# Stores and job loads of one stage issued from GpSimd's DMA queue instead of SyncE's, in a gated FNet and Mish kernel

## The chip, the cores and the metric

The kernel runs on one core of one Trainium2 chip. The metric is the device time of one execution in microseconds (us). Three runs of the kernel before took 877.42, 878.73 and 881.01 us, so the median is 878.73 us.

## What is computed

The input `x` has 2048 rows of 640 columns, float32. One branch mixes it with Fourier matrices, the other is a dense layer, Mish and a second dense layer. A gate per row joins them:

```python
g = _sigmoid((x * gate_w).sum(-1, keepdims=True))
# branch A
a = jnp.einsum("bsd,ed->bse", x, dft_hid_re)
b = jnp.einsum("bsd,ed->bse", x, dft_hid_im)
y = jnp.einsum("ts,bse->bte", dft_seq_re, a) - jnp.einsum("ts,bse->bte", dft_seq_im, b)
# branch B, F = 1728
h = jnp.einsum("bsd,df->bsf", x, w1) + b1
act = h * jnp.tanh(softplus(h))
b = jnp.einsum("bsf,fd->bsd", act, w2)
return g * a_branch + (1 - g) * b
```

## The kernel before

**Arithmetic.** Each float32 operand is split into a high part (a copy on ScalarE, `copy`, L96) and a low part (a subtraction on VectorE, `tt`, L93), both in fp32r. A product is three matmuls of 128x128 by 128x512 (`mm3`, L107): high by high, high by low, low by high. The matrix products use Strassen-like block sums, so VectorE also adds and subtracts blocks of the operands and of the results.

**Stages.** The whole work is one list of `steps`, each of some 3 to 25 matmuls, built in Python in this order: the product with the sequence matrices (`seq`), the product with the hidden Fourier matrices (`hid`), the first dense layer, the second dense layer (`out`). The first dense layer, here "dense first stage", is steps `nd` = 336 to `n_dense` - 1 = 429. Counted in the order of the program, where the matmuls stand in the trace too, it is the matmuls 2,280 to 3,009 of 3,757. It starts with 13 steps of `dense_quads` (L866) and 8 of `dense_rest` (L768), then come two rounds of `dense_first` (L932), one for each half of the rows. `dense_quads` writes partial results to scratch tensors in device memory (names `p1_...`, `p2_...`, in the trace `p`), `p_load` (L973) reads them back some steps later. The activations go to the scratch tensors `act` and `actr`, and the `out` stage reads them.

**What a step needs.** A step names operands to load (`raw`), and preparations (`preps`, the split). The loop at L1239 goes through the steps. At step i it first issues the loads of operands of steps a few ahead (L1250; in the dense stages 6 steps for the preparation and 4 more for the load), then the preparations, then the matmuls of step i, then the stores that are due (L1259), and then whatever jobs fit.

**Jobs.** Work that isn't bound to one step stands in a list `jobs`, in a fixed order: low parts of weights, the gate, sums of blocks of `x` (`x_sum_jobs`, L855), weights of the dense layers (`quad_job` L660, `w1_job` L695), the multiplication of the Fourier branch by the gate (`yg`), the multiplication of the last activations by 1 - g (`aq`), weights of the second layer. A job has a load part and a work part. The loads are issued by the loop at L1286 when buffers are free, from the step `first` on at the earliest. The work part begins some steps later (L1282), and goes on as long as a planned clock of VectorE is behind a planned clock of TensorE by a margin (L1279). The six jobs of `x_sum_jobs` each load four blocks of `x`, make four sums on VectorE and store them to scratch tensors (`xs`, `q0s`, `q1s` in the trace); the dense first stage loads them as operands. Their `first` is `XS_FIRST + XS_EACH * n`, so 160, 168 and so on to 200. The trace has their first store at 285 us, in step 185.

**Buffers.** `FS` holds 22 tiles `f` of 128x512 float32 (256 KB), `FX` four tiles `fx` of 128x640, `W` the split weights, `R` the split operands. `Slots.get` takes the tile that has been free longest. A tile that is stored goes back to the list as soon as its store is issued in the plan; whoever takes it next then waits on the chip for that store to land. The Tile framework puts in these waits, and those for data, as semaphores.

**Queues.** Nearly all DMAs are issued by SyncE (SP), in the order in which the plan reaches them: operands at L1250, stores at L1259, loads of jobs into `fx` tiles at L154 (`fx_load`) and L692 (`quad2_load`), loads of jobs and of partial results into `f` tiles at L159 (`fs_load`) and L244 (`top_load`). SP works through its instructions in order: a store whose tile VectorE has not finished, or a load whose tile is not free yet, holds up all that stand behind it. ScalarE issues two loads at the start and one store near the end. GpSimd (POOL) issues no DMA and computes next to nothing.

Of the kernel before, what the change touches and what calls it, by code (L numbers as in the profile page):

```python
# [12 lines left out]
S, D, F = 2048, 640, 1728  # L13
P = 128
# [25 lines left out]
P2_LOAD, C_SEED = 4, 4  # L40
OPS0, OPS1 = (2, 7, 9, 11), (-4, 0, 2, 4, 5, 6, 8)
YG_FIRST, NO_LOAD = 18, 3
LATE_Y = (0,)
XS_FIRST, XS_EACH = 160, 8
R0, R1 = (2, 4), (2, 4)


# [14 lines left out]
def fnet_mish_gate(ctx: ExitStack, tc: tile.TileContext, xn, xt, c_re, c_im, wd_re, wd_im,  # L62
                   w1a, w1b, b1a, b1b, w2, gw, out):
    nc = tc.nc
# [13 lines left out]
    def scratch(name, n, rows=P):  # L78
        return [[dr.tile([rows, N], F32, name=f"{name}{i}_{t}") for t in range(TG)] for i in range(n)]

    usc, ysc = scratch("u", 2 * KD), scratch("y", KD)
    g_row, q_row = (dr.tile([1, S], F32, name=n) for n in ("g", "q"))
    gsc, qsc = ([r[:, t * N:(t + 1) * N].to_broadcast([P, N]) for t in range(TG)] for r in (g_row, q_row))
    asc = scratch("act", FC) + [[dr.tile([FR, N], F32, name=f"actr_{t}") for t in range(TG)]]

    clock = {"pe": 0.0, "dve": 0.0, "step": 0}
# [31 lines left out]
    A2, B2 = slice(0, 2 * P), slice(2 * P, 4 * P)  # L118
# [9 lines left out]
    def at(i, fn):  # L128

        events.setdefault(i, []).append(fn)  # L130
# [14 lines left out]
    def simple(fn):  # L145
# [3 lines left out]
            yield  # L149
        return work  # L150

    def fx_load(src, width=D):
        f = FX.get()
        nc.sync.dma_start(f if width == D else f[:, :width], src)  # L154
        return f

    def fs_load(src):
        f = FS.get()
        nc.sync.dma_start(f[:src.shape[0]], src)  # L159
        return f  # L160

    def job_load(i):
        j = jobs.pop(0)
        loaded.append((j, j.load(), i))

    def job_start():
        j, a, _ = loaded.pop(0)
        running.append((j.key, j.work(*a)))

    def job_go():  # L170
        key, work = running[0]
        pause = next(work, None)
        if pause is None:
            running.pop()
            done_jobs.add(key)
        return pause or 0
# [60 lines left out]
    def stage_jobs(st, order):  # L237
        def do_top(k, g):
            top(st, k, g[:, :3 * P])
            FS.put(g)  # L240

        def top_load(k):
            g = FS.get()
            nc.sync.dma_start(g[:, :3 * P], st.row(k)[:, :3 * P])  # L244
            return [g]

        for what, k in order:
            if what == "top":
                jobs.append(Job((st.kind, "top", k), simple(lambda g, k=k: do_top(k, g)),
                                lambda k=k: top_load(k), (st.kind, k) not in tops, fs=1))  # L250
            else:
                jobs.append(Job((st.kind, "low", k), lambda g, f, k=k: low(st, k, g, f),
                                lambda k=k: [fx_load(st.row(k + st.kh)), fs_load(st.row(k)[:, P:])],
                                2 + (k % KD == 0) + ((st.kind, k) not in tops), 1, 1))
            tops.add((st.kind, k))
# [82 lines left out]
    class Problem:  # L338
# [52 lines left out]
        def second(self):  # L391
# [96 lines left out]
            if self.out:  # L488
                for t in (t1, t2):
                    at(n - 2, lambda t=t: QT.update({t: fs_load((gsc if t in LATE_Y else qsc)[t])}))  # L490
                self.y_load(done - 5, t2, 4)
# [111 lines left out]
        def give(self, d, t, f):  # L603
            if self.out:
                y = YT.pop((d, t))
                if t in LATE_Y:

# [81 lines left out]
    def quad2_load(g):  # L689
        f = FX.get()  # L690
        for i in range(2):
            nc.sync.dma_start(f[:, i * 2 * P:(i + 1) * 2 * P], w1a[2 * g + i][:, B2])  # L692
        return [f]

    def w1_job(f, ga, gb):  # L695
# [440 lines left out]
    def put_u(m):  # L1136
        return lambda d, t, f: store(usc[m * KD + d][t], f, f)
# [9 lines left out]
    hid = Stage("hid", KD, lambda k: (wd_re, wd_im)[k // KD][k % KD], neg=True)  # L1147
    fin = Stage("out", FP, lambda k: w2[k * P:(k + 1) * P])

    def aside(name):  # L1150
        return [dr.tile([P, N], F32, name=f"{name}{j}") for j in range(3)]

    sq = [Problem(seq, q // 2, lambda t, k, m=q % 2: (c_re, c_im)[m][t, k], put_u(q % 2), q == 3,
                  aside(f"ps{q}") if q in (1, 2) else None) for q in range(4)]
    hd = [Problem(hid, tp, lambda t, k: usc[k][t], put_y, tp == 1, aside("ph") if tp else None) for tp in range(2)]
    ou = [Problem(fin, tp, lambda t, k: asc[k][t], put_out, False, aside("po") if tp else None) for tp in range(2)]

    unwritten.update(id(d) for p in problems for d in p.s2)

# [7 lines left out]
    def yg_jobs(*ts):  # L1167
        for t in ts:
            for d in range(KD):
                jobs.append(Job(("yg", t, d), simple(lambda *a, t=t, d=d: gate_y(t, d, list(a))),  # L1170
                                lambda t=t, d=d: ([fs_load(gsc[t])] if d == 0 else []) + [fs_load(ysc[d][t])], fs=2))

    def aq_jobs():
        for t in (3, 2):
            jobs.append(Job(("aq", t), simple(lambda *a, t=t: act_q(t, *a)),
                            lambda t=t: [fs_load(d) for d in (qsc[t], asc[FC - 1][t], asc[FC][t])], fs=3))

    yg_jobs(*[t for t in (0, 1) if t not in LATE_Y])
    aq_jobs()
# [18 lines left out]
    nd = len(steps)  # L1198
# [12 lines left out]
    narrow.update(range(nd, len(steps)))  # L1211
    quiet = set(range(nd - 4, nd + QUIET)) | set(range(nm + QUIET_A, nm + QUIET_M))
    n_dense = len(steps)
    no_load = set(range(n_dense - 3, n_dense + NO_LOAD))
    ou[0].first(ks=range(3))
    ou[1].first()
# [16 lines left out]
    def spare(i, job=False):  # L1233

        return SPARE + (SPARE_D * job if i in narrow else (i >= n_dense) * SPARE_OUT) + sum(takes.get(i + j, 0) for j in range(5))
# [3 lines left out]
    for i in range(n_all):  # L1239
        clock["step"] = i  # L1240
        while ready < n_all and ready <= i + (LEAD_D if ready in narrow else LEAD):
            while li < len(loads) and loads[li][0] <= ready + (AHEAD_D if loads[li][0] in narrow else AHEAD):
                n, (key, src) = loads[li]
                if n > ready and len(FS.free) <= spare(i):
                    break
                if id(src) in unwritten or id(src) in late and n >= n_dense and late[id(src)] not in done_jobs:
                    assert n > ready, (n, ready, i, key)
                    break
                f = RAW[key] = FS.get()
                nc.sync.dma_start(f[:src.shape[0], :src.shape[1]], src)  # L1250
                li += 1
            for prep in steps[ready][1]:
                prep()
            ready += 1
        clock["dve"] = max(clock["dve"], clock["pe"] - 3)
        steps[i][2]()
        while stores and stores[0][3] <= i:
            dst, v, f, _ = stores.pop(0)
            nc.sync.dma_start(dst, v)  # L1259
            FS.put(f)  # L1260
            unwritten.discard(id(dst))
        if steps[i][3]:
            steps[i][3]()
        for fn in events.get(i, ()):
            fn()
        if i == nm + GIVE_AT:
            lent = len(extra) - GIVE
        for r, w in list(extra) if i >= nm + GIVE_AT else ():
            if len(extra) > (NB if i >= n_dense - BACK else lent) and any(r is o for o in R.free):
                R.free = [o for o in R.free if o is not r]  # L1270
                extra[:] = [e for e in extra if e[0] is not r]
                W.put(w)
        if i == 20:
            nc.sync.dma_start(b1s[:, :FC], b1a)
            nc.sync.dma_start(b1s[:FR, FC:], b1b)
        if not (jobs or loaded or running):
            while FX.free:
                FS.put(FX.get()[:, :N])
        while clock["dve"] < clock["pe"] + (SLACK_D if nd <= i < nm + D_END else SLACK if ("seq", "low", KH - 1) in done_jobs else SLACK_UP) and i >= wait_until and i not in quiet:  # L1279
            if running:  # L1280
                wait_until = i + job_go()
            elif loaded and loaded[0][2] + (J_WAIT if i in narrow else 3) <= i and len(W.free) >= loaded[0][0].w:  # L1282
                job_start()
            else:
                break
        while i not in no_load and jobs and len(loaded) < (NLOAD if i in narrow else 2) and len(FX.free) >= jobs[0].fx and i >= jobs[0].first and (i in narrow and not jobs[0].fs or len(FS.free) >= jobs[0].fs + spare(i, True)):  # L1286
            job_load(i)
# [48 lines left out]
```

## Time and profile before

| | us |
|---|---|
| runs of the kernel before | 877.42, 878.73, 881.01 (median 878.73) |
| profiled execution, its own time | 883.24 |
| its span, from the first to the last instruction | 881.4 |
| TensorE (PE) busy / weight loads (PEld) | 863.3 / 710.3 |
| VectorE (DVE) busy | 742.3 |
| ScalarE (ACT) busy | 504.9 |
| GpSimd (POOL) busy | 0.2 |
| DMA | 244.43 MB, mean 277 GB/s |

PE's busy time counts matmuls that overlap in a pipeline, so its share says little by itself; a matmul of 128x128 by 128x512 is shown as 391 ns long, and the next one starts about 227 ns after it. A line such as `L105` is the place in the kernel that issued the instruction, and since one helper (`mm`, `copy`, `tt`) records every operation of a kind, the names of the tiles tell more than the line. `SPq` rows are instructions of SyncE's sequencer; what stands behind an arrow ended the wait before it.

### The profile page before, as it was taken

The page shows a single profiled execution, that of the slowest core. Times are in us where ns is not written, and L with a number is a line of the kernel's source. Part 1 is how long each engine was busy: PE and PEld are TensorE (multiplying, and loading weights), DVE is VectorE, ACT ScalarE, POOL GpSimd, SP SyncE. Part 2 cuts the span into 40 slices and gives each one's busy share as a digit, 9 for nine tenths or more (in the row PEclk, how much of TensorE's full clock was granted, in tenths as well). Part 3 has the DMA queues.
Part 4 walks back from the last instruction along what each step waited for, and adds up shares of the span by engine and source line. Part 5 has one row for each costly group of instructions (what it writes and reads, how often), then busy time and mean ns, then how long its engine had stood idle before and what let it go on. Part 6 is the DMA issues. An engine that isn't in the chain of part 4 may idle for free.

```text
span 881.4 us, 12420 instructions
## 1 busy us (share of the span) xinstructions
PE 863.3 (98%) x3757; PEld 710.3 (81%) x3757; DVE 742.3 (84%) x1301; ACT 504.9 (57%) x938; POOL 0.2 (0%) x4
## 2 busy tenths in 40 slices
PE   9999999999999999999999999799899999999998
PEld 7888888888888888888888888588787787888786
DVE  6999998898879778998999788686568849999993
ACT  6756636545463444657666578575575737743442
POOL 0000000000000000000000000000000000000000
PEclk9999999999999999999999999899999999999999
DMA  9985848886768999887869798888999587595952
GB/s 348 333 266 195 260 157 305 286 281 224 276 201 268 314 360 370 277 292 280 290 219 371 239 327 295 293 281 301 365 382 395 180 276 250 182 334 161 356 197 107
DMA packets 133603, 244.43 MB, mean 277 GB/s; under 512 B 15392, under 2 KB 18720, under 8 KB 133536
## 3 DMA queue, kind: packets, MB, share of 16 engines
q1 hardware_dynamic: 133104, 242.99, 80.3%
q8 instruction: 29, 0.48, 0.2%
q10 hardware_dynamic: 432, 0.66, 0.2%
q14 instruction: 38, 0.31, 0.1%
HBM read 185.38 MB, written 58.21 MB: 276 GB/s over the span
## 4 chain that ended last, share of the span: by engine, by line
PE 72%; DVE 11%; DMA 10%; issue 3%; ACT 2%; SPq 2%; DVEq 0%; ACTq 0%
PE ps L105 72%; DVE f L93 5%; DVE wl L93 3%; DVE rl L93 2%; DMA f<-act 2%; DMA act<-f 1%; DMA y<-f 1%; DMA fx<-in_w_dram 1%; SPq L1250 1%; DVE fx L93 1%; DMA fx<-in_w1a_dram 1%; ACT wh L96 1%; DMA fx<-act 1%; DMA f<-xs 1%; DMA f<-q1s 1%
## 5 line engine op out<-in xcount | busy, mean ns | idle before, releaser
L105 PE MATMUL ps<-rh,wh 128*128 128x512 f32 (+1 forms) x1080 | 421.8, 392 | 11.3 <-DVE f L93 8.3
L105 PE MATMUL ps<-rl,wh 128*128 128x512 f32 x1063 | 415.1, 391 | 2.3 <-DVE rl L93 2.3
L105 PE MATMUL ps<-rh,wl 128*128 128x512 f32 x1061 | 413.5, 391 | 0.0
L96 ACT ACTIVATE rh<-f 128x512 fp32r<-128x512 f32 (+1 forms) x427 | 255.9, 627 | 182.1 <-DVE f L93 92.1
L93 DVE TENSOR_TENSOR rl<-f,rh 128x512 fp32r<-128x512 f32 x425 | 278.1, 686 | 55.4 <-ACT rh L96 54.3
L105 PEld LDWEIGHTS ps<-rh,wh 128*128 128x128 f32 x1080 | 203.9, 189 | 56.7 <-DVE f L93 6.5
L105 PEld LDWEIGHTS ps<-rl,wh 128*128 128x128 f32 x1063 | 200.9, 189 | 44.9 <-DVE rl L93 3.5
L105 PEld LDWEIGHTS ps<-rh,wl 128*128 128x128 f32 x1061 | 200.3, 189 | 41.8
L93 DVE TENSOR_TENSOR f<-f,f 128x512 f32<-128x512 f32 (+1 forms) x318 | 216.3, 689 | 9.4 <-DMA q0s<-f 2.1
L96 ACT ACTIVATE f<-ps 128x512 f32<-128x512 f32 (+1 forms) x162 | 92.8, 596 | 70.6 <-PE ps L105 58.1
L96 ACT ACTIVATE wh<-f 128x512 fp32r<-128x512 f32 (+3 forms) x156 | 72.5, 502 | 45.4 <-DVE f L93 36.0
L93 DVE TENSOR_TENSOR wl<-f,wh 128x512 fp32r<-128x512 f32 (+3 forms) x155 | 78.2, 536 | 16.2 <-ACT wh L96 16.0
L93 DVE TENSOR_TENSOR f<-ps,f 128x512 f32<-128x512 f32 x100 | 65.1, 685 | 16.0 <-PE ps L105 10.7
L105 PE MATMUL ps<-wh,wh 128*128 128x512 f32 x184 | 72.4, 394 | 0.0
L105 PE MATMUL ps<-wh,wl 128*128 128x512 f32 x181 | 70.9, 392 | 0.0
L105 PE MATMUL ps<-wl,wh 128*128 128x512 f32 x179 | 70.4, 393 | 0.0
L93 DVE TENSOR_TENSOR wl<-fx,wh 128x640 fp32r<-128x640 f32 (+4 forms) x68 | 39.7, 612 | 17.3 <-ACT wh L96 17.1
L96 ACT ACTIVATE wh<-fx 128x640 fp32r<-128x640 f32 (+5 forms) x69 | 36.6, 565 | 22.3 <-DVE fx L93 8.7
L766 ACT ACTIVATE f<-f,b1s 128x512 f32<-128x512 f32 x36 | 25.4, 719 | 31.6 <-DVE f L93 31.5
L105 PEld LDWEIGHTS ps<-wh,wh 128*128 128x128 f32 x184 | 35.0, 190 | 7.7 <-DVE f L93 0.3
L105 PEld LDWEIGHTS ps<-wh,wl 128*128 128x128 f32 x181 | 34.4, 190 | 7.2
L105 PEld LDWEIGHTS ps<-wl,wh 128*128 128x128 f32 x179 | 34.0, 190 | 7.4 <-DVE wl L93 0.2
(35 smaller groups left out, 175.7 us busy)
## 6 DMA issues: line engine op xcount, KB each, us to landing
f<-in_c_re_dram SPq DMA_DIRECT2D x128, 256.0 KB, 4.1
f<-in_c_im_dram SPq DMA_DIRECT2D x128, 256.0 KB, 4.7
f<-act SPq DMA_DIRECT2D x93, 256.0 KB, 4.8
f<-u SPq DMA_DIRECT2D x70, 256.0 KB, 4.8
f<-in_xt_dram SPq DMA_DIRECT2D x54, 256.0 KB, 4.9
act<-f SPq DMA_DIRECT2D x54, 256.0 KB, 4.9
u<-f SPq DMA_DIRECT2D x40, 256.0 KB, 3.6
y<-f SPq DMA_DIRECT2D x35, 256.0 KB, 5.3
```

The lines of the kernel that those rows point to most:

```text
L93: nc.vector.tensor_tensor(o, a, b, op=op)
L96: nc.scalar.activation(o, a, AF.Copy, scale=scale)
L105: nc.tensor.matmul(ps, a, b, start=start, stop=stop, skip_group_check=True)
L766: nc.scalar.activation(o[rows], src[rows], AF.Mish, bias=b1s[rows, f:f + 1])
L1250: nc.sync.dma_start(f[:src.shape[0], :src.shape[1]], src)
```

## The change

From step `nd` up to `n_dense`, stores (L1259) and the loads of `fx` tiles (L154 and L692) are issued on GpSimd's queue instead of SP's. Loads of operands (L1250), loads of `f` tiles (`fs_load`, `top_load`) stay on SP. Before step `nd` and from `n_dense` on everything is issued as before. The first job of the sums of `x` may be loaded from step 140 on instead of 160, the following ones 10 steps apart instead of 8. The old helper `aside`, which made scratch tensors, is only renamed to `three`.

```diff
-XS_FIRST, XS_EACH = 160, 8
+XS_FIRST, XS_EACH = 140, 10
...
+    def aside():
+
+        return nc.gpsimd if len(span) == 2 and span[0] <= clock["step"] < span[1] else nc.sync
+
+    span = []
+
     def fx_load(src, width=D):
         f = FX.get()
-        nc.sync.dma_start(f if width == D else f[:, :width], src)
+        aside().dma_start(f if width == D else f[:, :width], src)
         return f
...
     def quad2_load(g):
         f = FX.get()
         for i in range(2):
-            nc.sync.dma_start(f[:, i * 2 * P:(i + 1) * 2 * P], w1a[2 * g + i][:, B2])
+            aside().dma_start(f[:, i * 2 * P:(i + 1) * 2 * P], w1a[2 * g + i][:, B2])
         return [f]
...
     n_dense = len(steps)
+    span += [nd, n_dense]
...
         while stores and stores[0][3] <= i:
             dst, v, f, _ = stores.pop(0)
-            nc.sync.dma_start(dst, v)
+            aside().dma_start(dst, v)
             FS.put(f)
```

More of the change, by code (lines that the diff above doesn't have):

```diff
@@ L1148, in fnet_mish_gate, with three @@
     fin = Stage("out", FP, lambda k: w2[k * P:(k + 1) * P])
-    def aside(name):
+    def three(name):
         return [dr.tile([P, N], F32, name=f"{name}{j}") for j in range(3)]
     sq = [Problem(seq, q // 2, lambda t, k, m=q % 2: (c_re, c_im)[m][t, k], put_u(q % 2), q == 3,
-                  aside(f"ps{q}") if q in (1, 2) else None) for q in range(4)]
-    hd = [Problem(hid, tp, lambda t, k: usc[k][t], put_y, tp == 1, aside("ph") if tp else None) for tp in range(2)]
-    ou = [Problem(fin, tp, lambda t, k: asc[k][t], put_out, False, aside("po") if tp else None) for tp in range(2)]
+                  three(f"ps{q}") if q in (1, 2) else None) for q in range(4)]
+    hd = [Problem(hid, tp, lambda t, k: usc[k][t], put_y, tp == 1, three("ph") if tp else None) for tp in range(2)]
+    ou = [Problem(fin, tp, lambda t, k: asc[k][t], put_out, False, three("po") if tp else None) for tp in range(2)]
     unwritten.update(id(d) for p in problems for d in p.s2)
```

## Prediction

> **What bounds the kernel now.** I read the page first: TensorE is busy in nearly the whole span, so only the places where it isn't can give time. Then I cut the span by matmuls (busy time by windows). The columns are PE, weight loads (PEld), DVE, ACT, POOL with their counts, the granted clock, the DMA share and GB/s. The cuts lie where a run of matmuls breaks off or is whole again; 519.58 and 704.26 are the starts of the stage's first matmul (the 2,280th) and of the first one behind it.
>
> ```profile
> 100.00:500.00 400.00, 400.00 (x1766) 331.33 (x1765) 350.31 (x596) 223.68 (x401) 0.00 (x0) 1.00 0.83 282
> 519.58:552.45 32.87, 32.87 (x147) 27.22 (x145) 26.36 (x49) 26.69 (x54) 0.00 (x0) 1.00 0.89 315
> 552.45:582.85 30.40, 24.49 (x94) 19.35 (x93) 19.38 (x37) 16.50 (x33) 0.00 (x0) 0.89 0.88 301
> 582.85:631.61 48.76, 48.60 (x214) 39.90 (x213) 33.43 (x65) 31.68 (x62) 0.00 (x0) 1.00 0.90 308
> 631.61:642.31 10.70, 8.05 (x29) 6.13 (x27) 6.22 (x10) 6.08 (x10) 0.00 (x0) 0.84 1.04 395
> 642.31:694.12 51.81, 51.32 (x226) 42.15 (x225) 41.18 (x75) 34.01 (x65) 0.00 (x0) 1.00 0.97 356
> 694.12:704.26 10.14, 8.04 (x29) 6.12 (x27) 8.86 (x16) 6.80 (x14) 0.00 (x0) 0.83 0.37 129
> ```
>
> From 100 to 500 us a matmul starts every 400 / 1766 = 0.2265 us and PE never idles: there nothing is to be won. The stage that the change touches has 145 + 93 + 213 + 27 + 225 + 27 = 730 weight loads, so 730 matmuls, which at 0.2265 us would take 165.3 us. It takes 704.26 - 519.58 = 184.7 us and so loses 19.3 us, 2.2% of the span of 881.4 us. By stretch, time minus count x 0.2265: 0.0, 9.3, 0.5, 4.6, 0.8 and 4.0 us. Three stretches hold 17.9 of it, and in each the clock falls too (0.89, 0.84, 0.83): a gap costs itself and a slow spell behind it.
>
> What ended the gaps, by the timelines of PE, ACT and DVE (in brackets: idle time before, and the releaser):
>
> ```profile
> 531.24 0.60 ACT L96 ACTIVATE f<-ps 128x512 f32<-128x512 f32 x1 [1.31 <-DMA y<-f]
> 532.91 1.16 DVE L93 TENSOR_TENSOR wl<-fx,wh 128x512 fp32r<-128x512 f32 x2 [2.99 <-ACT wh L96]
> 557.73 0.47 PE L105 MATMUL ps<-rh,wh 128*128 128x512 f32 x1 [3.08 <-DVE f L93]
> 565.79 0.63 ACT L96 ACTIVATE wh<-f 128x512 fp32r<-128x512 f32 x1 [5.05 <-DMA f<-q1s]
> 566.96 0.79 PE L105 MATMUL ps<-rh,wh 128*128 128x512 f32 x1 [2.83 <-ACT f L96]
> 633.79 1.29 ACT L96 ACTIVATE rh<-f 128x512 fp32r<-128x512 f32 x2 [0.92 <-DMA f<-xs]
> 636.46 0.50 PE L105 MATMUL ps<-rh,wh 128*128 128x512 f32 x1 [2.65 <-DVE f L93]
> ```
>
> The three gaps of PE here start from transfers: a slot whose `y` store landed late, an operand `q1s` that came late, an operand `xs` that came late. Why they were late stands in SP's own timeline:
>
> ```profile
> 521.76 3.46 SPq L1250 DMA_DIRECT2D f<-in_xt_dram  x5
> 525.34 1.62 SPq L1259 DMA_DIRECT2D y<-f  x3
> ...
> 529.88 4.08 SPq L154 DMA_DIRECT2D fx<-in_w1a_dram  x2
> 534.07 0.37 SPq L1250 DMA_DIRECT2D f<-q0s  x1
> ...
> 550.67 3.56 SPq L154 DMA_DIRECT2D fx<-in_w1a_dram  x2
> 554.28 0.45 SPq L1259 DMA_DIRECT2D actr<-f  x1
> 554.78 0.58 SPq L1259 DMA_DIRECT2D act<-f  x1
> 555.40 1.47 SPq L1259 DMA_DIRECT2D p<-f  x3
> 556.91 1.13 SPq L159 DMA_DIRECT2D f<-p  x1
> 558.14 1.98 SPq L1259 DMA_DIRECT2D p<-f  x3
> 560.22 0.67 SPq L159 DMA_DIRECT2D f<-p  x1
> 560.93 1.69 SPq L1250 DMA_DIRECT2D f<-q1s  x3
> ...
> 620.18 2.41 SPq L1259 DMA_DIRECT2D act<-f  x3
> ...
> 628.55 1.13 SPq L1250 DMA_DIRECT2D f<-xs  x2
> ```
>
> Each queue entry stands behind waits that are not its own: the `y` stores behind five loads, the `q0s` load behind a pair of weight loads of which the second waits for its tile, the `q1s` loads behind eight stores and that pair, the `xs` loads behind a run of stores. SP's waits in the stage (us in total, times, longest), and then the issues by line with KB each and the median time to landing:
>
> ```profile
> SPq L1259 <- DVE f L93: 26.1, 31, 6.9
> SPq L154 <- DVE wl L93: 16.2, 9, 3.2
> ```
>
> ```profile
> act<-f SPq DMA_DIRECT2D x49, 256.0 KB, 4.9
> p<-f SPq DMA_DIRECT2D x24, 256.0 KB, 3.4
> ```
>
> **The change part by part.** It moves 99 stores (49 `act`, 6 `actr`, 24 `p`, 20 `y`) and 16 loads of `fx` tiles, 115 DMAs in all by the plan's steps 336 to 429, from SP to POOL, which has nothing else to do (0.00 in all rows). SP keeps some 100 loads. No DMA, byte or computation is added, and the waits themselves stay; what changes is who stands behind them. The 26.1 and 16.2 us that stores and weight loads wait for DVE no longer hold loads of operands.
>
> *First gap* (of the 9.3 us, 3.2 are lost from 552.45 to 557.73: 5.28 us for 9 matmuls). The `y` stores of 525.34 would go at about 521.8, when the five loads ahead of them began; with the time that the chain of waits has for the landing, below, they land near 527.6, before ACT needs the slot at 531.24 - 1.31 = 529.9. Then DVE's 2.99 us idle before 532.91 goes, and with it about 3 us of the lateness that PE meets at 557.73. Gain 3.2.
>
> ```profile
> 525.34 5.82 DMA y<-f
> ```
>
> *Second gap* (6.1 of the 9.3 us, slow spell included). The `q1s` loads lose the stores ahead of them, but not the `f<-p` load of 560.22: it reads back what the first `p` store of 555.40 wrote, which now lies in the other queue, behind the same weight loads and two stores, and its landing must be waited for at the head of SP's queue. Before, that store landed after 3.4 us, near 558.8, and the `q1s` loads went 2.1 us later. So at most 2.1 of the 2.83 us gap close, with the slow spell perhaps all of it; if POOL takes longer per DMA than SP, nothing closes. Between 0 and 6.1 I take half, 3.0.
>
> *Third gap* (4.6 us). The `xs` loads could go at about 620 instead of 628.55. But here the DMA engines are full (share 1.04, 395 GB/s), and loads that are ahead share them with the stores that they passed. Half again, 2.3.
>
> *Fourth gap* (4.0 us): nothing. DVE is at 8.86 of 10.14 us there and the DMA share is 0.37, so it is DVE's own backlog of weights for the last stage.
>
> *What POOL costs.* A DMA issued by POOL is not in this trace. Below, it can't beat SP's issue of the same shape; the row is a store that had waited, 0.32 us. Above, the worst is that POOL takes one DMA after the other to its landing, 4.9 us.
>
> ```profile
> 696.40 0.32 SPq L1259 DMA_DIRECT2D act<-f  x1
> ```
>
> 115 x 0.32 = 37 us fits in the stage four times; 115 x 4.9 = 563 us would be a disaster; the point between is 184.7 / 115 = 1.6 us. I go by the near row, the same instruction on another queue, and allow it three times that, 1.0 us: 115 us of POOL in 184.7. In bursts (three stores in 1.5 us at 555.40) that makes a store land some 2 us later than now, and its slot comes back so much later. For this I charge 2.5 us, about half of a gap such as the third. The same price, up to a whole gap, is the cost if the cover, slots that are free anyway, is missing.
>
> The DMAs run on the same engines whoever issues them. The Trainium skill, "DMA: Bandwidth & Descriptors", section "Issuing engines are not separate DMA queues", says that issuing from several engines only saves the sequencer's issue time, which is usually small. By it the change gives nearly nothing. The rows above speak against it in so far as SP's time is lost in waits, not in issuing, and for it in the third gap.
>
> *Jobs of x's sums.* The six jobs have 24 loads and 24 stores of 256 KB, 12.6 MB. They may start at step 140 (223 us) in place of the 179th, where the plan had tiles for them, and so leave a crowded stretch (DMA share 0.95 here) for an emptier one.
>
> ```profile
> 223.00:281.00 58.00, 58.00 (x258) 48.04 (x257) 49.27 (x80) 29.10 (x51) 0.00 (x0) 1.00 0.74 249
> 281.00:342.00 61.00, 61.00 (x271) 50.53 (x270) 48.09 (x78) 28.20 (x48) 0.00 (x0) 1.00 0.95 332
> ```
>
> PE is full in both, so this gains nothing by itself. It is hidden by DVE's 8.7 idle us of 58; without that cover each of the 24 sums costs at most a DVE addition. Zero.
>
> Sum: 3.2 + 3.0 + 2.3 - 2.5 = 6.0 us. The profiled execution took 883.24 us (span 881.4 and 1.8 around it), 4.5 more than the median of the runs, 878.73. I take the 6.0 us off both: 877.2 there, **872.7 us** for the median.
>
> **The rivals.** *All three gaps go* (chance 0.10): loads run so far ahead that neither the read-back nor the full DMA engines matter. Then 9.3 + 4.6 = 13.9 us go, 864.8; with the fourth too, 860.8. Against it: the read-back is in the plan.
>
> *Hidden anyway* (0.25): the read-back of `p` keeps the second gap, full engines keep the third, and what the first gives is lost in late slots. 3.2 - 2.5 = 0.7 us gain, 878.0; within 4.4 us of before, either way. For it: DMA shares of 0.88 to 1.04 in all stretches but the last.
>
> *POOL becomes the bound* (0.18): slower. Price and place: if writing a DMA takes POOL more than 1.6 us, stores come out at its rate, slots return at that rate, and the stage stretches; at 1.8 us it takes 207 us, 22.3 more, 901. It could come about if POOL can only work beside an idle DVE: DVE is busy 26.36 + 19.38 + 33.43 + 6.22 + 41.18 + 8.86 = 135.4 of 184.7 us, which leaves 49.3 us, 0.43 per DMA. Against it: nothing in the trace shows POOL waiting for DVE, as it does nothing.
> The Trainium skill, "SBUF — State Buffer", section "SBUF: two separate sides", has a form of this: a DVE operation in a two-port mode keeps GpSimd from writing descriptors. It excepts tensor_tensor, the operation of DVE's rows above, for writes; by that rule this rival falls, which no row here can show.
>
> *Late slots* (0.07): slower. A slot's next user waits for a store that POOL issued late, at several places instead of one: two more gaps as large as the third, 9.2 us, against 8.5 gained in the sum without its charge, and the `f<-p` loads at the head of SP's queue late each time. It decides from about 2 us later landing on; 883 to 885.
>
> **How the numbers follow.** A measurement here can tell about 0.5%, 4.4 us, from no change. The forecast, a gain of 4.4 to 10 us, has 0.40, all gaps 0.10: faster 0.50. Hidden anyway 0.25: same. POOL and slots 0.25: slower. The range leaves out most of the first rival and the far part of POOL's: 864 to 885. The forecast's own range is 868.7 to 874.3. The lowest price of POOL lies inside; the highest, 4.9 us each, is left to the chance outside.
>
> **What would show it.** Right: no 3 us gap at the stage's 146th matmul; `q0s` loads issued in one run, without pairs of weight loads between; SP's waits for DVE near zero, and POOL's queue with the 42 us instead; a POOL issue of some 1 us. If the second gap stays and its chain runs from a `p` store over `f<-p` to `q1s`, the read-back was the bound. The forecast is wrong if PE's gaps lie at new places with SP waiting for `act` or `p` stores (slots), if POOL's issues follow one another without a pause (POOL's bound), or if PE, gapless now from 100 to 500 us, loses time between 223 and 350 us (x's sums).

## The result and the profile after

20 runs of the changed kernel have a median of 878.58 us (875.21 to 880.40), 20 runs of the kernel before on the same chip one of 878.81 (875.03 to 883.49). The ratio is 0.9996, 95% interval 0.9982 to 1.0011: no change. The forecast of 872.7 was wrong by 5.9 us; the rival "hidden anyway" (878.0) came nearest; of what it described only the second gap, kept by the read-back, came about.

The page of the changed kernel, its busy times and its DMA queues (packets, MB, share of 16 engines):

```profile
PE 861.0 (98%) x3757; PEld 708.8 (81%) x3757; DVE 742.1 (85%) x1301; ACT 504.6 (58%) x938; POOL 62.9 (7%) x119
...
q1 hardware_dynamic: 116928, 212.71, 71.0%
q0 software_dynamic: 9008, 30.28, 9.3%
```

The change did what it says: 115 DMAs of 30 MB went to POOL's queue q0, and POOL's busy time went from 0.2 to 62.9 us. Its price stands in the groups of instructions of the dense first stage (busy us, mean ns of one, then the waits before them):

```profile
L1267 POOL DMA_DIRECT2D act<-f x49 | 26.7, 546 | 58.7 <-DVE f L94 32.8 <-ACT f L773 20.1 <-ACT wh L97 3.5
L1267 POOL DMA_DIRECT2D p<-f x24 | 13.0, 544 | 19.9 <-DVE f L94 16.9 <-ACT f L97 2.1 <-issue 0.3
...
L161 POOL DMA_DIRECT2D fx<-in_w1a_dram x10 | 5.5, 553 | 23.9 <-DVE wl L94 23.7
```

0.55 us each, some 63 us in a stage of 180: POOL is no bound. Now the gaps. PE's and ACT's timelines and the windows (length, then busy us of PE, PEld, DVE, ACT, POOL, PE's granted clock, DMA share, GB/s) answer to the rows of before:

```profile
556.58 0.47 PE L106 MATMUL ps<-rh,wh 128*128 128x512 f32 x1 [2.57 <-DVE f L94]
567.73 0.50 PE L106 MATMUL ps<-rh,wh 128*128 128x512 f32 x1 [3.13 <-ACT f L97]
```

```profile
566.56 0.63 ACT L97 ACTIVATE wh<-f 128x512 fp32r<-128x512 f32 x1 [6.26 <-DMA f<-q1s]
```

```profile
551.81:582.41 30.60, 24.90 (x94) 19.61 (x93) 18.88 (x36) 16.50 (x33) 13.03 (x24) 0.89 0.88 295
582.41:628.00 45.59, 45.43 (x200) 37.28 (x199) 32.82 (x64) 31.30 (x61) 16.89 (x31) 1.00 0.93 350
628.00:638.00 10.00, 10.00 (x45) 8.02 (x44) 6.99 (x12) 6.60 (x12) 4.35 (x8) 1.00 1.04 403
```

The third gap is gone: from 628 to 638 us PE is busy 10.00 of 10.00 at full clock. The first is nearly as before (2.57 us in place of 3.08). The second is there with the same chain, and worse: ACT waits 6.26 us for `q1s` instead of 5.05. Why, is in SP's and POOL's timelines:

```profile
543.30 15.14 SPq L166 DMA_DIRECT2D f<-p  x2
558.52 4.70 SPq L1258 DMA_DIRECT2D f<-q1s  x3
```

```profile
549.79 0.55 POOL L161 DMA_DIRECT2D fx<-in_w1a_dram  x1 [5.33 <-DVE wl L94]
553.01 0.55 POOL L161 DMA_DIRECT2D fx<-in_w1a_dram  x1 [2.67 <-DVE wl L94]
553.55 0.55 POOL L1267 DMA_DIRECT2D actr<-f  x1
554.09 0.58 POOL L1267 DMA_DIRECT2D act<-f  x1
554.66 1.61 POOL L1267 DMA_DIRECT2D p<-f  x3
556.73 1.74 POOL L1267 DMA_DIRECT2D p<-f  x3 [0.47 <-DVE f L94]
```

SP reaches the two `f<-p` loads at 543.30 already and then stands for 15 us, because a store of `p` that one of them reads back goes out only at 554.66: on POOL it is behind two weight loads that wait for DVE. The three `q1s` loads behind it go at 558.52 to 563.22 (before from 560.93), and then take long to land: 8.2 us in the median (before 5.1). The rows for `q1s` from 540 to 575 us, before and then after:

```profile
DMA to landing us min/median/max: 4.8/5.1/6.0
```

```profile
DMA to landing us min/median/max: 4.1/8.2/8.8
```

SP's waits by cause in the stage (us in total, times, longest) show the exchange. Before, stores and weight loads held SP with 26.1 and 16.2 us of waits for DVE; now it is the landing of stores in the other queue, for a slot or for what is read back:

```profile
SPq L166 <- DMA act<-f: 30.2, 15, 7.0
SPq L1258 <- DMA act<-f: 26.6, 6, 14.0
SPq L166 <- DMA p<-f: 22.6, 8, 9.0
```

For the comparisons I use the time that PE loses per step: from a step's first matmul to the next one's, less 0.227 us per matmul. Steps with over 0.3 us lost, summed by place (us); steps 427 to 429 lose 3.8 to 4.0 in all of them, but where noted:

| kernel | steps 349-351 | 352-354 | 380-393 |
|---|---|---|---|
| before, execution shown | 3.2 | 6.0 | 4.6 |
| before, a second one | 5.1 | 1.6 | 6.3 |
| after | 4.5 | 5.0 | 0 |
| only stores moved | 4.4 | 0 | 0 (2.6 at 427-429) |
| only weight loads moved | 5.6 | 0 | 4.9 |
| after, `p` read back on POOL | 2.7 | 0 | 0 |
| after, `p` stores on SP | 4.4 | 1.2 | 0 |
| after, `p` loaded 3 steps later | 2.7 | 0 | 0 (7.4 at 427-429) |
| after, fewer sums on DVE | 1.9 | 8.6 | 0 |

### The profile page after: what moved, and what is told of

It is laid out like the page before. It is cut to its first block, busy times and chain, and to the rows that moved or that the text cites. A ratio compares the mean times of both kernels' runs of the same rounds, so it can differ in the third digit from the quotient of the medians.

```text
span 876.3 us, 12547 instructions
## 1 busy us (share of the span) xinstructions
PE 861.0 (98%) x3757; PEld 708.8 (81%) x3757; DVE 742.1 (85%) x1301; ACT 504.6 (58%) x938; POOL 62.9 (7%) x119
## 4 chain that ended last, share of the span: by engine, by line
PE 74%; DVE 10%; DMA 6%; issue 5%; ACT 3%; POOL 1%; SPq 1%; DVEq 0%; POOLq 0%; ACTq 0%
PE ps L106 74%; DVE f L94 4%; DVE rl L94 2%; DVE wl L94 2%; ACT f L97 1%; ACT rh L97 1%; DMA f<-q1s 1%; DMA f<-act 1%; DVE fx L94 1%; DMA act<-f 1%; POOL act L1267 1%; DMA y<-f 1%; DMA f<-xs 1%; DMA f<-in_w_dram 1%; ACT wh L97 1%
## 5 line engine op out<-in xcount | busy, mean ns | idle before, releaser
L97 ACT ACTIVATE rh<-f 128x512 fp32r<-128x512 f32 x424 | 254.2, 626 | 171.3 <-DVE f L94 94.2
L94 DVE TENSOR_TENSOR wl<-f,wh 128x512 fp32r<-128x512 f32 (+3 forms) x159 | 80.5, 538 | 22.6 <-ACT wh L97 22.4
L106 PE MATMUL ps<-wl,wh 128*128 128x512 f32 x186 | 72.5, 390 | 1.5 <-DVE wl L94 1.5
L1267 POOL DMA_DIRECT2D y<-f x20 | 11.0, 550 | 530.3 <-DVE f L94 529.3
```

The lines of the kernel that those rows point to most:

```text
L94: nc.vector.tensor_tensor(o, a, b, op=op)
L97: nc.scalar.activation(o, a, AF.Copy, scale=scale)
L106: nc.tensor.matmul(ps, a, b, start=start, stop=stop, skip_group_check=True)
L1267: aside().dma_start(dst, v)
```

## The experiments

My theory: splitting the queues frees the operands at the third gap, and gives the gain back at the second, since the read-back of `p` at SP's head now waits for a store that stands behind weight loads in POOL's queue. Rivals: x's sums; DVE's backlog; the mere second queue, whose packets make SP's loads land late; a third gap that was an accident of one execution.

**The kernel before once more** (no edit).

> The kernel before, once more, for a second trace. If the third gap (4.6 us lost at 632 us in the first trace) is an accident of that execution: the first two gaps again cost 9 to 10 us together, the fourth 4.0, and there is nothing near matmul 2,730; span 876 to 878 us. If it belongs to the kernel and the two queues cured it: a loss of 4 to 5 us there again, span near 881.

881.0 us (span 879.2). The third gap is there again, 6.3 us, while the second is 1.6 instead of 6.0: so the third is no accident of one execution (the two further kernels with their stores on SP, below, have it as well, 4.8 and 5.0 us), and the second varies from execution to execution. Both executions of before lie above the median of its runs (883.24 and 881.0 against 878.8 to 879.9), so their gaps are somewhat larger than those of a middling run.

**The read-back off SP's head.**

```diff
-            KEEP[("p1", "p2")[n], f] = fs_load(qout[n][f][tp])
+            g = KEEP[("p1", "p2")[n], f] = FS.get()
+            nc.gpsimd.dma_start(g, qout[n][f][tp])
```

> The changed kernel, with the loads of the partial results (f<-p) on GpSimd's queue too. Read-back theory (the q1s loads stand behind an f<-p load that waits for its store to land): the three q1s loads go some 8 us earlier or more, the second gap closes with its slow spell, 4 to 5 us faster, near 874; the first gap stays. Backlog theory (both gaps come from DVE's and ACT's program order, loaded with the jobs of w1): within 1 us of the changed kernel, 878.

872.36 us (871.84 to 874.02), ratio to before 0.9925 (0.9903 to 0.9946). SP's timeline:

```profile
541.67 7.30 SPq L1259 DMA_DIRECT2D f<-q1s  x4
```

All four `q1s` loads are issued by 548.97, 9.5 us before three of them began in the changed kernel; they land after 3.2 us (median), and the second gap is gone. The stores and weight loads on POOL are as in the changed kernel, so neither a second queue nor POOL's issue price was what kept the gain.

**The read-back 3 steps later.**

```diff
-P_LOAD, P_SEED = 8, -1
+P_LOAD, P_SEED = 5, -1
```

> The changed kernel, with the first loads of partial results three steps later (P_LOAD 5 instead of 8), so behind the q1s loads in SP's order. Read-back theory: as in p_on_pool, 4 to 5 us faster, near 874. Backlog theory: within 1 us of the changed kernel; some loss is possible where a seed then waits for its partial result.

877.34 us (876.0 to 877.87), ratio 0.9978 (0.9965 to 0.9991). The second gap closes here too, but the edit holds for every round of `p`, and at step 427, where 2.3 us were lost, it is now 5.4:

```profile
691.59 0.80 PE L106 MATMUL ps<-rh,wh 128*128 128x512 f32 x1 [5.25 <-DVE f L94]
```

Most of the gain was given back at another place, so the total says little on the theory; the second gap's end does.

**DVE's backlog.** In the weight jobs of f = 1, 2, 3 the four block sums are left out (`add` does nothing there but keep the plan's clock).

```diff
+        add = skip if f in (1, 2, 3) else tt
-        tt(ga[:, A2], gb[:, A2], ga[:, A2], OP.subtract)
+        add(ga[:, A2], gb[:, A2], ga[:, A2], OP.subtract)
...
```

> The changed kernel without the four block sums on DVE of the weights w1 of blocks 1 to 3 (left out, with the plan's clock advanced as if they ran). Backlog theory: two of these jobs, 8 operations of 0.42 us, lie before the first gap, which shrinks by about its whole 2.6 us and takes its slow spell along; 3 to 4 us faster, near 875. Read-back theory: the first gap's DVE releaser was waiting for transfers, so nothing changes by more than 1 us.

880.4 us (879.27 to 880.87), ratio 1.001 (0.9999 to 1.0022): with less work for DVE no faster. The first gap shrank, PE's wait from 2.57 to 1.77 us, and the second grew to 8.6 lost us, since its end is set by `q1s`, whose loads leave SP at 559.33. A gap that is shortened ahead of a later one with its own date is paid back there.

**x's sums from step 160 as before**, queues split.

```diff
-XS_FIRST, XS_EACH = 140, 10
+XS_FIRST, XS_EACH = 160, 8
```

> The changed kernel with x's sums from step 160, 8 apart, as before; only the queues are split. Theory that the early sums are worth nothing (PE is full in their stretch): as the changed kernel, 878.6, ratio 0.998 to 1.002, the same gaps. Rival, that the early sums take something at the stage's beginning (slots or DVE time): first gap below 2.7 us and the time down by up to 1 us, unless the second gap takes it back, as it did without the sums of f = 1 to 3; rival on the other side, that they relieve the crowded stretch: 1 to 3 us slower, PE idle between 281 and 350 us.

879.36 us (877.92 to 882.2), ratio 1.0014 (0.9998 to 1.0031). This and the changed kernel's interval overlap; steps 349 to 354 lose 4.5 and 4.7 us, as in the changed kernel. No effect of the earlier sums can be told.

**The two moves apart.** Stores alone on POOL (`nc.sync` again in `fx_load` and `quad2_load`), and weight loads alone on POOL (`nc.sync` again for the stores):

```diff
-        aside().dma_start(f if width == D else f[:, :width], src)
+        nc.sync.dma_start(f if width == D else f[:, :width], src)
...
-            aside().dma_start(f[:, i * 2 * P:(i + 1) * 2 * P], w1a[2 * g + i][:, B2])
+            nc.sync.dma_start(f[:, i * 2 * P:(i + 1) * 2 * P], w1a[2 * g + i][:, B2])
```

```diff
-            aside().dma_start(dst, v)
+            nc.sync.dma_start(dst, v)
```

> The changed kernel with its sixteen loads of fx tiles back on SP; the 99 stores stay on POOL. Read-back theory: p stores no longer stand behind weight loads that wait for DVE, so they land earlier and the f<-p loads at SP's head wait less than the 15.1 us of the changed kernel; but the operand loads stand behind the weight loads again, so of the second gap's 6 to 7 us about half goes: 875 us, ratio 0.993 to 0.998. The third gap stays away, as the run of stores that held the xs loads is still on POOL. Rival, that a second queue as such costs what it gains (loads land later beside POOL's larger packets): 878 to 880, second gap as in the changed kernel. A third one, that only the loads' move removed the third gap, would show that gap again, some 4 us at step 391.

> The changed kernel with its 99 stores back on SP; only the sixteen loads of fx tiles go on POOL. Read-back theory: stores and read-back are in one queue again, in order, so the second gap is as in the kernel before, 1.6 to 6 us, or smaller, since the q1s loads no longer stand behind a weight load; the run of act stores before the xs loads is back, so the third gap of 4.6 to 6.3 us is back too: 877 to 880, ratio 0.998 to 1.001. Rival, that the weight loads' waits for DVE were what held the operands: second and third gap both gone, 868 to 871.

Stores alone: 871.94 us (871.44 to 872.83), ratio 0.9931 (0.9914 to 0.9949). Weight loads alone: 878.91 (875.37 to 880.91), ratio 1.0001 (0.9986 to 1.0015). So the whole gain is in the stores, and the weight loads, worth nothing by themselves in the time, take it back when they go to the same queue. (In the one trace with the weight loads alone the second gap is away too, but the first is larger, 5.6 us, and the third is there.) Of what the stores alone gain, 1.4 us are at the fourth gap: steps 427 to 429 lose 2.6 instead of 4.0, as the slow spell behind that gap is missing (the granted clock is 1.00 there, from 683 to 698 us, where it is 0.83 in the changed kernel). Why, was not tried. POOL's and then SP's timeline of the kernel with the stores alone:

```profile
551.51 1.62 POOL L1267 DMA_DIRECT2D p<-f  x3 [2.20 <-DVE f L94]
```

```profile
549.58 3.55 SPq L161 DMA_DIRECT2D fx<-in_w1a_dram  x2
553.23 1.22 SPq L166 DMA_DIRECT2D f<-p  x2
554.50 1.56 SPq L1258 DMA_DIRECT2D f<-q1s  x3
```

Without the weight loads ahead the `p` stores go at 551.51, not 554.66; the `f<-p` loads take 1.22 us, and `q1s` goes 4.0 us earlier than in the changed kernel and lands after 5.3 us. SP still waits for the weight loads (up to 553.13 here), but what stands behind them now can afford it. More went than the half of the second gap that I expected: all of it.

With the weight loads alone the third gap is back, in windows and in PE's timeline:

```profile
627.68:638.64 10.96, 8.02 (x28) 6.14 (x27) 6.79 (x11) 6.19 (x10) 0.00 (x0) 0.84 1.04 390
```

```profile
632.82 0.50 PE L106 MATMUL ps<-rh,wh 128*128 128x512 f32 x1 [2.94 <-DVE f L94]
```

The DMA engines are as full here (1.04, 390 GB/s) as in the changed kernel without the gap (1.04, 403). So full engines don't keep that gap. It is there with the stores on SP and away with them on POOL, alone or with the weight loads; that it is the run of `act` stores ahead of the `xs` loads, and not another of the 99 stores, is read from SP's timeline and was not tried by itself.

**The read-back alone**: the edit of the second experiment in the kernel before.

> The kernel before with only the f<-p loads issued on POOL; all else stays on SP. Read-back theory: in one queue the f<-p load waits only 1 to 2 us, since the store of p went just ahead of it, so its move saves about 2 us at the second gap and nothing at the third: 876 to 878, ratio 0.997 to 0.999. Rival, that moving the read-back is the whole gain and the split of stores and loads is worth nothing: as the kernel with both, 872, ratio 0.9925.

881.35 us (878.52 to 884.2), ratio 1.003 (1.0012 to 1.0047): slightly slower, where I had expected a small gain. The third gap stays (5.0 us). The rival that the read-back is the whole of it falls: its move is worth something only where stores and loads are in two queues. Its trace loses 1.7 us at steps 365 and 367, where no other trace does; why, I did not follow up.

**The `p` stores in the queue of their read-back**, the rest as in the changed kernel.

```diff
-            aside().dma_start(dst, v)
+            (nc.sync if any(dst is o for r in qout[0] + qout[1] for o in r) else aside()).dma_start(dst, v)
```

> The changed kernel with only the 24 p stores back on SP, in the queue of the loads that read them back; weight loads and the other stores stay on POOL. Theory that the p stores were late because they stood behind weight loads that wait for DVE in POOL's queue: the p store goes 2 to 3 us earlier and the f<-p load's wait at SP's head falls from 15.1 us to some 3 us, the second gap goes, the third stays away: 871 to 873, ratio 0.990 to 0.994. Rival, that the weight loads on POOL make SP's loads land late whatever the order (q1s took 8.2 us to landing in the changed kernel, 5.3 without them): second gap stays at 3 us or more, 876 to 879.

875.23 us (873.76 to 877.19), ratio 0.9943 (0.9923 to 0.9963): between the two numbers, and SP's timeline corrects my theory:

```profile
556.42 1.52 SPq L1267 DMA_DIRECT2D p<-f  x3
558.04 0.69 SPq L166 DMA_DIRECT2D f<-p  x1
558.78 1.52 SPq L1258 DMA_DIRECT2D f<-q1s  x3
```

The wait of the read-back is gone, but now the second group of `p` stores, which waits for DVE, stands at SP's head, and `q1s` goes no earlier than in the changed kernel (558.78 against 558.52). Still 3.8 of the second gap's 5.0 lost us go. What differs is the landing, 5.0 us in the median instead of 8.2. From 556 to 566 us, the queues of the changed kernel first (packets, MB, share of 16 engines), then those of this one:

```profile
q0 software_dynamic: 796, 2.56, 81.0%
q1 hardware_dynamic: 399, 0.74, 19.5%
...
f<-q1s SPq DMA_DIRECT2D x3, 256.0 KB, 8.4
```

```profile
q1 hardware_dynamic: 1417, 2.59, 79.0%
q0 software_dynamic: 228, 0.71, 18.6%
...
f<-q1s SPq DMA_DIRECT2D x3, 256.0 KB, 4.7
```

Both moved 3.30 MB. In the changed kernel POOL's queue had 78% of it, seven `p` stores that run beside `q1s`; SP's loads got 22%. In one queue `q1s` came next behind those stores and landed sooner. So the second gap has two parts: loads issued late, and late because of the read-back; and loads that go just when POOL's stores take the DMA engines. Issued 4 us earlier (stores alone) they are ahead of the second group of `p` stores, which goes at 556.79 there.

**Is it the size of POOL's packets?** In q0 a packet has 3.4 KB in the mean, in q1 1.8.

```diff
-    qout = [[[dr.tile([P, N], F32, name=f"p{n + 1}_{f}_{tp}") for tp in range(2)] ...
+    qout = [[[dr.tile([P, N + 64], F32, name=f"p{n + 1}_{f}_{tp}")[:, :N] for tp in range(2)] ...
```

> The changed kernel, unchanged but for the scratch tiles of p in DRAM, whose rows get 64 unused elements behind the 512, so that two rows no longer lie end to end. From 556 to 566 us of the changed kernel POOL's queue moved 2.56 MB in 796 packets (3.2 KB each), SP's 0.74 MB in 399 (1.9 KB), and q1s took 8.2 us to landing. Theory that POOL's larger packets take the DMA engines from SP's: packets of p stores fall to 2 KB, the shares come near each other, q1s lands in 5 to 6 us, and up to 3 us of the second gap goes: 875 to 877.5, ratio 0.995 to 0.998. Rival, that it is how much POOL's queue has outstanding and not its packets' size: q1s 7.5 us or more, 878 to 879.5. A third, that packets stay at 3 KB whatever the rows: no difference in packets, nothing is told.

878.45 us (877.65 to 879.91), ratio 0.9982 (0.9967 to 0.9998), and on the page:

```profile
q0 software_dynamic: 9008, 30.28, 9.3%
```

The same packets to the last one, and the second gap stays (7.2 us lost): the third outcome, nothing is told. Whether it is packet size or what a queue has outstanding that takes the DMA engines stays open.

**Both cures together**: stores and read-back on POOL, weight loads on SP.

> Stores on POOL, weight loads on SP, and the f<-p loads on POOL too. Theory that the two edits take away the same wait (the p store's landing at SP's head): they don't add up, and the time is that of either alone, 871.9 to 872.4, or at most 1.7 us less, the 0.85 us each that is left at steps 350 and 351: 870 to 872.4, ratio 0.990 to 0.993. Rival, two separate gains of some 6.5 us each that add up: 866. Rival on the other side, that the weight loads on SP hold the operands once nothing else does: 874 to 877, with PE waiting for q0s or q1s.

875.45 us (872.53 to 877.5), ratio 0.995 (0.993 to 0.9969). They don't add up. The interval overlaps those of either alone (0.9914 to 0.9949 and 0.9903 to 0.9946), so whether both together are worse can't be told from the ratios, but the trace shows new losses. The second gap is away, and even the slow spell at steps 350 and 351 (0.85 us each), but 1.8 us are lost between steps 380 and 393 and 1.9 more at 441 and 442. SP's waits for landed `act` stores, before operand loads, of this kernel and then of the one with the stores alone:

```profile
SPq L1259 <- DMA act<-f: 34.7, 9, 15.8
```

```profile
SPq L1258 <- DMA act<-f: 24.5, 5, 14.0
```

Now the `f<-p` loads, which wait, stand ahead of `act` stores in POOL's queue, so the third rival came about in part, though by another wait. That these waits make the new losses is argued from the two rows, not shown.

**DVE's backlog without the read-back behind it**: stores alone on POOL, and the sums left out as above.

> Stores alone on POOL, and four block sums of DVE left out in each of the weight jobs of f = 1, 2, 3 (work left out, so the output is not the reference's). What is left of the first gap is 2.73 us at step 349, with DVE without a pause from 549.6 to 556.5. Theory that it is DVE's backlog: it shrinks to 1.9 us or less, as it did without these sums in the changed kernel, and with no read-back behind it the time falls as well: 869 to 871. Rival, that it is the late slot of a y store, as the prediction had it: 2.73 us stays, 871.5 to 872.5. A third, that the next wait takes it back as in the changed kernel: gap 1 smaller, steps 350 to 353 longer, same time.

871.08 us (870.49 to 872.34), ratio 0.9899 (0.9868 to 0.993). PE's timeline:

```profile
555.71 0.47 PE L109 MATMUL ps<-rh,wh 128*128 128x512 f32 x1 [1.77 <-DVE f L94]
```

1.77 us in place of 2.57, and 1.93 lost at step 349 in place of 2.73; the slow spell at 350 and 351 goes too. So the first gap depends on DVE's work. The time's own interval overlaps that of the stores alone, so by the time alone a gain can't be told.

## Why the prediction was wrong

**Two steps failed: the second gap's term, and the base.**

*The second gap's term*, "Between 0 and 6.1 I take half, 3.0". It named the right wait: the `p` store in the other queue "behind the same weight loads", its landing awaited at SP's head. Its date for the loads held too: SP is past the read-back at 558.44 (forecast near 558.8), and the `q1s` loads go from 558.52 on, 2.4 us earlier than before (forecast 2.1). What failed is the next step, that loads issued earlier arrive as much earlier. The landing was taken as unchanged, while beside POOL's stores it went from 5.1 to 8.2 us: ACT has its first `q1s` tile at 566.56, where it was 565.79 before. Steps 350 to 354 lost 6.7 us instead of 6.0, so the term is -0.7 and not 3.0. Nothing was not the worst end, and the weight loads that moved along are the reason that the loads go no earlier still: without them the `p` store goes at 551.51 in place of 554.66, and the gap is away. (The second execution of before lost only 3.3 us at these steps; against it the change made this gap worse.)

*The base*, "I take the 6.0 us off both", is the larger part of the miss. The traced execution went from 883.24 to 878.04 us, near the 877.2 that the prediction gave for it; the median went down by 0.2. The profiled execution was 4.4 us above the median, and I took the gain off both, as if a middling run had gaps as large. By the shown execution the three places lost 13.8 us before and 9.4 after, a gain of 4.4; by the second one 13.0 and 3.6. Both are above the median. The whole stage loses 19.3 us in the first trace of before, 18.6 in the second and 15.1 after, and what is left of the span is 862.1, 860.6 and 861.2 us. So, by an estimate from these numbers, an execution of before at the median (878.81 us, span 877.0) loses 15 to 16 us in the stage, about what the changed kernel loses. The mean granted clock, lower with each slow spell, agrees: 0.992 in both traced executions of before, but 0.995 in the median of 91 others, of which 15 are at 0.992 or below; 0.994 in the median of the changed kernel's 20. Which of its gaps a middling execution of before lacks, no trace shows.

That the number for the traced execution came out within 0.8 us is luck: the first gap's term was 2.7 us too high and the second's 3.7, the third's 2.3 too low, and the charge of 2.5 did not show.

**Third gap**, "Half again, 2.3": the mechanism was right, the size wrong. All 4.6 us went (6.3 in the other execution). "But here the DMA engines are full" was no reason: they are full with and without the gap.

**First gap**, "Gain 3.2": step 349 lost 2.7 us instead of 3.2, a gain of 0.5. The late slot went as forecast: the `y` stores go at 519.83 (POOL's timeline), earlier than the forecast 521.8, and the activation that waited for its slot until 531.24 is now the last of three that run on from 528.40 (ACT's). But DVE's pause of 2.99 us only shrank to 1.55, as the third row, DVE's, shows, and little of that came through to PE:

```profile
519.83 1.75 POOL L1267 DMA_DIRECT2D y<-f  x3 [519.38 <-DVE f L94]
```

```profile
528.40 1.58 ACT L97 ACTIVATE f<-ps 128x512 f32<-128x512 f32 x3
```

```profile
531.03 1.16 DVE L94 TENSOR_TENSOR wl<-fx,wh 128x512 fp32r<-128x512 f32 x2 [1.55 <-ACT wh L97]
```

PE's wait, which ends at 556.58, fell from 3.08 to 2.57 us only. Just before it DVE has no pause; its timeline in the kernel with the stores alone, where PE's wait of 2.57 us ends at 556.64:

```profile
549.62 0.69 DVE L94 TENSOR_TENSOR rl<-f,rh 128x512 fp32r<-128x512 f32 x1
550.23 1.88 DVE L94 TENSOR_TENSOR f<-ps,f 128x512 f32<-128x512 f32 x3
552.02 1.22 DVE L94 TENSOR_TENSOR wl<-fx,wh 128x384 fp32r<-128x384 f32 x3
...
555.21 0.69 DVE L94 TENSOR_TENSOR rl<-f,rh 128x512 fp32r<-128x512 f32 x1
555.81 1.88 DVE L94 TENSOR_TENSOR f<-ps,f 128x512 f32<-128x512 f32 x3
```

Without some sums the wait shrinks to 1.77 us. So DVE's own work ends it, at least in part; what the other 1.77 us are was not tried.

**POOL's charge**, -2.5 by 1.0 us an issue: POOL takes 0.55. SP waits long for `act` stores to land (30.2 and 26.6 us in the rows above), but PE has no gap at a place where it had none before; the cost of the stores on POOL lies in what stands ahead of them and in the landing of the loads beside them. Then the rival that makes POOL the bound falls, and with it that POOL works only beside an idle DVE: from 628 to 638 us eight DMAs took 4.35 us of POOL while DVE was busy 6.99 of 10, so idle for 3.01. The Trainium skill, "SBUF — State Buffer", section "SBUF: two separate sides", excepts tensor_tensor from what keeps GpSimd from writing descriptors; the row agrees.

**x's sums**, nothing: holds within the overlap of the intervals. **Fourth gap**, nothing: holds, steps 427 to 429 lose 4.0 us before and after. **Late slots**, the rival: its two priced terms, 9.2 us against 8.5, give 879.4 and not 883 to 885; the rest was never worked out.

**The Trainium skill's rule**, "DMA: Bandwidth & Descriptors", section "Issuing engines are not separate DMA queues", by which issuing from several engines saves only the sequencer's time: for the change as it was made it gave the right result, but not the reason. The change's two parts measure 0.9931 (stores) and 1.0001 (weight loads) by themselves: who stands behind whom is worth 0.7% here, which the rule leaves out.

## What to carry to other kernels

Before a store is moved to another queue, look for the load that reads it back: that load now waits at the head of its own queue for the other one, with everything behind it. Work out the date of the store in its new queue, with all that is moved along with it and what that waits for; ask which loads run beside it and so land later; and never take zero as the worst end. Take a gain off the median only when an execution near the median shows the gaps that it comes from. Move one kind of transfer at a time: here the stores alone give 871.94 us, the stores with the weight loads 878.58.

## What the runs showed of the hardware

A DMA of 128x512 float32 takes POOL 0.55 us to issue, against 0.32 for the nearest row of SP. POOL's queue makes 80 packets of it, SP's 144: the packets in the traces are 64 of 4 KB and 16 of 4 bytes in q0, 128 of 2 KB and 16 of 4 bytes in q1. The 24 `f<-p` loads alone on POOL, on that kernel's page:

```profile
q0 software_dynamic: 1920, 6.29, 2.3%
```

The two queues did not share the DMA engines by halves: from 556 to 566 us of the changed kernel one had 2.56 MB and the other 0.74, and the other's loads landed after 8.4 us. The spread differs as well: 29 runs of before reach from 875.12 to 883.23 us, six of the stores alone on the same chip from 871.44 to 872.83; why, was not tried.
